# Column-tiled values and denominators in an attention and MLP kernel, with other first loads, a ring for the MLP input and warm-up matmuls

## The chip, the cores and the metric

The kernel runs on one core of a Trainium2 chip. The metric is the device time of one execution in microseconds (us); lower is better. The kernel before takes 539.99 us, the median of three runs (539.35 to 539.99).

## The reference

Eight sequences of 576 tokens go through attention with 8 heads of 64 and a bias that depends on the distance of two tokens (the bias table has 32 buckets for each head). The result, 4608 tokens of 512, goes through an MLP with a snake activation: 512 to 2048 and back to 512.

```python
scores = scale * np.matmul(q, k.transpose(0, 1, 3, 2))
scores = scores + bias_table[bucket].transpose(2, 0, 1)[None]
attn = np.exp(scores - max)
attn = attn / (np.sum(attn, axis=-1, keepdims=True) + 1e-09)
x = np.matmul(attn, v)              # heads side by side: 4608 x 512
h = x @ w_in
s = np.sin(alpha * h)
out = (h + s * s / (alpha + 1e-09)) @ w_out
```

## The kernel before

One stage per sequence t (0 to 7), in two parts. Scores are held transposed: keys on the partitions, queries along the row. In the code p is a pair of heads, z the head within the pair, w one of two windows of queries (384 and 192 wide) and c a chunk of 128 keys (c = 4 is the last 64 keys of both heads, stacked).

**Attention part.** For each pair p and window w, TensorE makes the scores (L472), ScalarE takes their exponential into u (L479), and VectorE multiplies the chunks near the diagonal by a table of exponentiated biases, m2 (L512), or mh for the last chunk (L495). Far from the diagonal the bias is one constant, which cancels. Then come values and denominators (L539): per head z, five matmuls over the key chunks. The stationary operand has 128 columns, 64 of values and 64 of ones, so that one accumulation gives the head's values on 64 rows and its denominator, copied 64 times, on the other 64. The two heads put them on opposite halves. ScalarE takes the logarithm of the denominators, one instruction of 64 rows per head (L553), and the exponential of its negative, one instruction of 128 rows (L566). VectorE multiplies the values by it into xT, one instruction of 64 rows per head (L574).

**MLP part.** A block b is 512 tokens; stage t does block t, and stage 7 does 7 and 8. For each of 16 groups f of 128 hidden units there are four matmuls (L600), a sine on ScalarE (L607), a square on ScalarE or VectorE (L614, L616), and the combination with h on VectorE into g (L621). The second matmul (L648, 64 per block, 16 for each of four outputs) needs a whole block of g. It is the fill: the planner puts its matmuls between the score matmuls of the next stage's attention. Exponential and sine need different tables on ScalarE, so each stage loads a table twice (L669).

**What sets the order.** Every engine works in its own order. A planner (class Plan) writes that order when the program is built: each task has costs, dependencies, a priority and, for some, an earliest time (T_V0, T_M2, T_W and so on), and the planner simulates the engines to choose. Fill matmuls are limited to QUOTA within the score matmuls of a stage. The simulated times choose the order only; on the chip an instruction waits for what it depends on.

**The start.** For t = 0 and t = 1 there is no time for the usual route of q and k (POOL writes them as f16 to DRAM, L273, and the DMA transposes them, L279 to L284). They are loaded with eight consecutive tokens in a row of 72 partitions (nat0 by SP at L321; nat1 and nat2 by POOL at L327 and L333), turned on TensorE (L396, L402) and copied out of PSUM by ScalarE or VectorE (L383, L385). In such a copy, neighbouring results go to places eight f16 elements apart, since eight tokens interleave. The bias table takes a chain: load the table (L314, L315), exponential (L350), a matmul with a 0/1 matrix phi_sb (L352), copy to e_sb (L353), and eight DMAs on SP that spread it over the partitions as m2, one per head (L355). VectorE builds mh from all heads of m2 (L372, L373). All the other loads go out on POOL's queue in the order of the program: q and k of t = 0, v of t = 0 (L291, L294), w_in (L301), q and k of t = 1, v of t = 1, and later w_out (L309), once the space of nat1 is free. The v tiles hold the ones beside the values, so that v is loaded in pieces of 64 columns.

## Time and profile before

| | |
|---|---|
| median of three runs | 539.99 us |
| the profiled execution | 541.17 us |
| its span, first to last instruction | 539.4 us |
| TensorE (matmul) busy | 452.9 us, 84% |
| ScalarE busy | 444.7 us, 82% |
| VectorE busy | 314.7 us, 58% |
| GpSimd busy | 100.6 us, 19% |
| first load of the exponential's table after stage 0 | at 124.08 us |
| the same after stage 6 | at 435.81 us |

A stage from 1 to 6 thus takes 51.96 us, stage 0 takes 124 us, and stage 7 with its two blocks takes 103.6 us. In the profile, a line number is one of the kernel before. A matmul's duration includes the way through the array, which the next matmul overlaps; how fast matmuls follow one another is read from a run of them. PE is TensorE, PEld its weight loads, ACT ScalarE, DVE VectorE, POOL GpSimd; SPq is the issuing of DMAs by SP.

### The profile page before, as it was taken

Reading aid. Unit: us, or ns where it says so; the run is one execution under the profiler, and the core shown is the slowest. Engines: PE = TensorE matmul, PEld = TensorE weight load, DVE = VectorE, ACT = ScalarE, POOL = GpSimd, SP = SyncE. Lnnn points to the kernel's source line nnn. Section 1 sums busy time; section 2 is a strip of 40 time slices with the busy share of each in tenths; the row PEclk is TensorE's granted clock in tenths of the full one; section 3 lists DMA queues with packets and bytes.
Section 4 is the critical chain, followed back from the end, with each engine's and each line's share of the span. In section 5 each row is a group of like instructions: output and inputs, shape, how many; then the busy total and the mean of one; then the engine's idle time right before and its main releaser. Section 6 shows DMA issues by size and latency. Waiting matters only on the chain.

```text
span 539.4 us, 7396 instructions
## 1 busy us (share of the span) xinstructions
PE 452.9 (84%) x2610; PEld 234.6 (43%) x2610; DVE 314.7 (58%) x613; ACT 444.7 (82%) x911; POOL 100.6 (19%) x114
## 2 busy tenths in 40 slices
PE   1414765399989998998999899979998999899997
PEld 0202442245544554454545444544554445444443
DVE  4623678276559555855675567557655765584800
ACT  3834777989989998999899989998998999895811
POOL 5334900710025004300520071005000000000000
PEclk9999776689999999999999999999999999999999
DMA  9999893990029904950694099309400000001022
GB/s 138 81 160 126 53 177 60 131 87 21 21 32 157 134 21 29 164 129 2 60 155 110 19 124 154 62 5 107 109 19 21 19 21 19 21 0 49 12 79 78
DMA packets 138977, 40.02 MB, mean 74 GB/s; under 512 B 125324, under 2 KB 133532, under 8 KB 138940
## 3 DMA queue, kind: packets, MB, share of 16 engines
q0 software_dynamic: 99072, 18.06, 44.1%
q1 hardware_dynamic: 39868, 21.49, 19.5%
q8 instruction: 20, 0.33, 0.3%
q14 instruction: 17, 0.14, 0.1%
HBM read 36.75 MB, written 16.52 MB: 99 GB/s over the span
## 4 chain that ended last, share of the span: by engine, by line
PE 53%; ACT 31%; DVE 6%; DMA 4%; SPq 3%; issue 2%; DVEq 0%; ACTq 0%
PE sc L600 24%; ACT u L479 20%; PE mo L648 14%; PE av L539 10%; PE sc L472 5%; ACT lnd L553 4%; SPq L355 3%; DMA m_73<-e_sb 3%; ACT rd L566 2%; ACT kz_67 L383 2%; DVE xT L574 2%; DVE kz_67 L385 2%; DMA phi_sb<-phi_const 1%; DVE u L512 1%; ACT L669 1%
## 5 line engine op out<-in xcount | busy, mean ns | idle before, releaser
L479 ACT ACTIVATE u<-sc 128x384 f16<-128x384 f32 x448 | 180.6, 503 | 3.1 <-PE sc L472 1.5
L648 PE MATMUL mo<-w_out_365,g 128*128 128x512 f16 x576 | 155.2, 379 | 0.0
L600 PE MATMUL sc<-xT,w_in_75 128*128 128x512 f16 x576 | 136.1, 386 | 6.3 <-DVE xT L574 6.3
L621 DVE SCALAR_TENSOR_TENSOR g<-sq,inv_a,sc 128x512 f16<-128x512 f16 x144 | 103.2, 745 | 17.0 <-ACT sq L614 7.5
L512 DVE TENSOR_TENSOR u<-u,m_73 128x512 f16<-128x512 f16 (+1 forms) x192 | 70.2, 392 | 66.7 <-ACT u L479 64.6
L574 DVE TENSOR_TENSOR xT<-av,rd 64x192 f16<-64x192 f32 (+1 forms) x128 | 58.2, 455 | 65.4 <-ACT rd L566 63.0
L600 PEld LDWEIGHTS <-w_in_75 128*128 128x128 f16 x576 | 57.0, 99 | 78.2 <-issue 16.8
L648 PEld LDWEIGHTS <-g 128*128 128x128 f16 x576 | 55.5, 97 | 64.4 <-issue 14.1
L472 PE MATMUL sc<-qT_69,kz_66 128*128 128x384 f16 (+1 forms) x288 | 65.5, 307 | 15.8 <-ACT u L479 15.3
L539 PE MATMUL av<-u,v_71 128*128 128x384 f16 (+1 forms) x320 | 56.2, 312 | 24.9 <-DVE u L512 21.1
L472 PE MATMUL sc<-qT_70,kz_67 128*128 128x384 f16 (+1 forms) x288 | 62.4, 284 | 12.1 <-ACT u L479 11.5
L553 ACT ACTIVATE lnd<-av 64x192 f32<-64x192 f32 (+1 forms) x128 | 51.8, 405 | 18.6 <-PE av L539 16.0
L291 POOL DMA_DIRECT2D v_72<-in_v_dram x32 | 24.0, 769 | 143.6 <-PE av L539 129.8
L539 PEld LDWEIGHTS <-v_71 128*128 128x128 f16 x320 | 31.2, 104 | 44.7 <-issue 30.1
L539 PE MATMUL av<-u,v_72 128*128 128x384 f16 (+1 forms) x320 | 49.3, 285 | 0.4 <-DVE u L512 0.2
L291 POOL DMA_DIRECT2D v_71<-in_v_dram x32 | 24.4, 788 | 114.8 <-PE av L539 110.3
L472 PEld LDWEIGHTS <-kz_66 128*128 128x128 f16 x288 | 28.9, 103 | 33.1 <-issue 20.6
L472 PEld LDWEIGHTS <-kz_67 128*128 128x128 f16 x288 | 27.4, 97 | 30.6 <-issue 16.4
L539 PEld LDWEIGHTS <-v_72 128*128 128x128 f16 x320 | 29.1, 97 | 18.3 <-issue 3.9
L383 ACT ACTIVATE outs<-mo 128x512 f32<-128x512 f32 x14 | 8.3, 595 | 26.2 <-PE mo L648 26.0
L566 ACT ACTIVATE rd<-lnd 128x384 f32<-128x384 f32 x64 | 27.9, 436 | 0.5
L383 ACT ACTIVATE kz_66<-mo 64x576 f16<-64x576 f16 (+2 forms) x5 | 10.9, 2269 | 19.0 <-DVE kz_66 L385 16.9
(345 smaller groups left out, 359.6 us busy)
## 6 DMA issues: line engine op xcount, KB each, us to landing
out_dram<-outs SPq DMA_DIRECT2D x36, 256.0 KB, 2.0
staged_k<-in_k_dram POOLq DMA_DIRECT2D x6, 576.0 KB, 9.5
staged_q<-in_q_dram POOLq DMA_DIRECT2D x6, 576.0 KB, 11.5
v_71<-in_v_dram POOLq DMA_DIRECT2D x32, 64.0 KB, 3.7
w_in_75<-in_moe_w_in_dram POOLq DMA_DIRECT2D x4, 512.0 KB, 17.1
v_72<-in_v_dram POOLq DMA_DIRECT2D x32, 64.0 KB, 5.4
w_out_365<-in_moe_w_out_dram POOLq DMA_DIRECT2D x4, 512.0 KB, 16.4
kz_66<-kraw SPq DMA_DIRECT2D x3, 288.0 KB, 3.6
```

Source lines behind the costliest of these rows:

```text
L291: nc.gpsimd.dma_start(out=dst[:, c], in_=vp[par, 128 * c : 128 * c + 128],)
L383: nc.scalar.activation(out=o, in_=i, func=AF.Copy)
L472: nc.tensor.matmul(out=sc.v[:, n * y : n * y + n], lhsT=kzs[t % 2][:, p, k0 : k0 + 128], rhs=qTs[t % 2][:, p, q0 : q0 + n], start=True, st ...
L479: nc.scalar.activation(out=u.v[:, k0 : k0 + nc_, q0 : q0 + n], in_=sc.v[:, 0 : n * nc_], func=AF.Exp, scale=0.125,)
L512: nc.vector.tensor_tensor(out=io, in0=io, in1=m2[:, 2 * p : 2 * p + 2, x0 : x0 + hi - lo], op=ALU.mult,)
L539: nc.tensor.matmul(out=avs[z].v[:, 0:n], lhsT=vs[t % 2][:, c, 2 * p + z, :, :], rhs=u.v[:, 8 if c == 4 else 4 * z + c, q0 : q0 + n], start ...
L553: nc.scalar.activation(out=ln.v[64 * z : 64 * z + 64, 0:n], in_=avs[z].v[64 - 64 * z : 128 - 64 * z, 0:n], func=AF.Ln,)
L566: nc.scalar.activation(out=rd.v[:, 0:n], in_=ln.v[:, 0:n], func=AF.Exp, scale=-1.0)
L574: nc.vector.tensor_tensor(out=xT[64 * z : 64 * z + 64, p, x0 : x0 + n], in0=avs[z].v[64 * z : 64 * z + 64, 0:n], in1=rd.v[64 * z : 64 * z ...
L600: nc.tensor.matmul(out=h.v, lhsT=w_in16[:, j, 128 * f : 128 * f + 128], rhs=xT[:, j, 512 * b : 512 * b + 512], start=(j == 0), stop=(j == 3),)
L621: nc.vector.scalar_tensor_tensor(out=gcell[b].v[:, f, :], in0=sq.v, scalar=inv_a[:, f : f + 1], in1=h.v, op0=ALU.mult, op1=ALU.add,)
L648: nc.tensor.matmul(out=m.v, lhsT=gcell[b].v[:, f, 128 * a : 128 * a + 128], rhs=w_out.v[:, f, :], start=(f == 0), stop=(f == NF - 1),)
```

## The change

1. **Bundles.** Per (t, p, w) there are two accumulations of both heads. The first gives the denominators on all 128 rows, the second the values. Each begins with a matmul of 128 columns for the stacked last chunk (ones2 or vh), and goes on with eight matmuls of 64 columns, alternately for the left and the right half of the array (z = 0, 1). A bundle is one task, and waits for all of its window's u. The logarithm becomes one instruction of 128 rows, and so does the multiplication into xT.
2. **First loads.** q and k of t = 0 and 1 have four tokens in a row: 128 partitions, and 16 for the last 64 tokens. A copy out of PSUM then writes four elements apart, and is two instructions (512 and 64 tokens). v needs no ones beside it and is loaded in six pieces instead of ten.
3. **Order of the loads.** phi_sb and the identity are loaded from ScalarE's queue. On POOL's queue come first pair 1 of q and k, the remainders, v, then pairs 2 and 3. Then POOL builds mh, and with it waits for m2; only behind it stand w_in, the loads for t = 1, and w_out, which has its own space now.
4. **Ring.** xT holds 1536 tokens instead of 4608; a multiplication that crosses the end is split.
5. **Warm-up.** Five matmuls on zeros ahead of the one of the bias table, and six behind it. The planner may add more in gaps; it adds none.
6. **Planner.** A change between bundles and other matmuls costs D_MODE there; fill has no gap, and its quota grows with the share of the scores done (8 + 48 times the share).

```diff
-        for z in range(2):
-            for c in range(4, -1, -1):
-                def mm(e, z=z, c=c):
-                    if c == 4:
-                        avs[z].v = new_av()
-                    nc.tensor.matmul(
-                        out=avs[z].v[:, 0:n], lhsT=vs[t % 2][:, c, 2 * p + z, :, :],
-                        rhs=u.v[:, 8 if c == 4 else 4 * z + c, q0 : q0 + n],
-                        start=(c == 4), stop=(c == 0),
-                    )
...
-            def lg(e, z=z):
...
-                nc.scalar.activation(
-                    out=ln.v[64 * z : 64 * z + 64, 0:n],
-                    in_=avs[z].v[64 - 64 * z : 128 - 64 * z, 0:n], func=AF.Ln,
-                )
+        for y in range(2):
+            def mm(e, y=y):
+                o = avs[y].v = new_av()
+                nc.tensor.matmul(
+                    out=o[:, 0:n], lhsT=vhs[t % 2][:, p] if y else ones2,
+                    rhs=u.v[:, 8, q0 : q0 + n], start=True, stop=False,
+                )
+                for c in range(4):
+                    for z in range(2):
+                        nc.tensor.matmul(
+                            out=o[64 * z : 64 * z + 64, 0:n],
+                            lhsT=vs[t % 2][:, c, 2 * p + z, :] if y else ones,
+                            rhs=u.v[:, 4 * z + c, q0 : q0 + n],
+                            start=False, stop=(c == 3),
+                        )
...
+            def lg(e):
+                ln.v = new_ln()
+                nc.scalar.activation(out=ln.v[:, 0:n], in_=avs[0].v[:, 0:n], func=AF.Ln)
...
-    SI = 8
-    SPB = S // SI
+    SI = 4
+    SN = (128, 16)
+    SO = (0, 512)
+    XN = 1536
...
+    nc.scalar.dma_start(out=phi_sb, in_=phi_h.ap())
+    nc.scalar.dma_start(out=id_sb, in_=idm.ap())
...
+    nc.gpsimd.tensor_copy(out=mh[0:64, :, :], in_=me[0:64, 0, :, 0:192])
+    nc.gpsimd.tensor_copy(out=mh[64:128, :, :], in_=me[64:128, 1, :, 64:256])
+    load_w_in16()
+    for kq, src in ((0, k), (1, q)):
+        load_nat([x[:, kq] for x in nat2], src[1], 0, H)
+    clear_v(nc.gpsimd, 1)
+    load_v16(1)
...
+    load_w_out16()
...
-FILL_GAP = 0.1
-QUOTA = 40
+D_MODE = 0.115
+FILL_GAP = 0.0
+QUOTA = 48
+OFFSET = 8
```

What stands on TensorE in a later stage. Before, values and denominators (L539, 128 columns) for the window of 192 stand between scores (L472) and fill (L648):

```order
L648 LDWEIGHTS g
L648 MATMUL mo<-w_out_365,g 128x512
L472 LDWEIGHTS kz_66
L472 MATMUL sc<-qT_69,kz_66 128x384
L539 LDWEIGHTS v_71
L539 MATMUL av<-u,v_71 128x192
```

Now a bundle begins; L607 is its matmul of 128 columns, L613 those of 64, of which eight follow one another:

```order
L541 LDWEIGHTS kz_67
L541 MATMUL sc<-qT_70,kz_67 128x384
L607 LDWEIGHTS ones_76
L607 MATMUL av<-u,ones_76 128x384
L613 LDWEIGHTS ones
L613 MATMUL av<-u,ones 64x384
```

And the place where the denominators' bundle ends and that of the values begins:

```order
L613 LDWEIGHTS ones
L613 MATMUL av<-u,ones 64x384
L607 LDWEIGHTS vh_74
L607 MATMUL av<-u,vh_74 128x384
L613 LDWEIGHTS v_72
L613 MATMUL av<-u,v_72 64x384
```

The matmuls of 128 columns that stood apart are now runs of eight of 64 columns, each run with one of 128 columns ahead of it. Of the 64 fill matmuls of a block, 61 stand among or ahead of the next stage's attention and 3 in the MLP part; before it was some 53 and 11.

POOL's queue at the start, before (v_71 and v_72 are v of t = 0 and 1, nat_89 is nat2):

```order
L294 DMA v_71<-in_v_dram 64x4x64 [waits DMASW3_49]
L301 DMA w_in_75<-in_moe_w_in_dram 128x2048 [waits DMASW4_49]
L301 DMA w_in_75<-in_moe_w_in_dram 128x2048 [waits DMASW5_49]
L301 DMA w_in_75<-in_moe_w_in_dram 128x2048 [waits DMASW6_49]
L301 DMA w_in_75<-in_moe_w_in_dram 128x2048 [waits DMASW7_49]
L333 DMA nat_89<-in_k_dram 72x8x512 [waits DMASW0_49]
```

And now (nat_128_95 is the part of nat1 with 128 partitions, nat_94 is nat2; DMAHW0 to 7 are the eight loads of m2):

```order
L346 DMA nat_128_95<-in_k_dram 128x4x256 [waits DMASW2_49]
L346 DMA nat_128_95<-in_q_dram 128x4x256 [waits DMASW3_49]
L413 COPY mh<-m_77 64x768 [waits DMAHW4_49,DMAHW6_49,DMAHW2_49,DMAHW0_49]
L414 COPY mh<-m_77 64x768 [waits DMAHW5_49,DMAHW7_49,DMAHW3_49,DMAHW1_49]
L354 DMA w_in_79<-in_moe_w_in_dram 128x2048 [waits DMASW4_49]
```

The load of w_in and all behind it now stand after the two copies that wait for m2.

286 lines of the change are left out of this document (164 added, 122 removed).

## The prediction

> **What bounds the kernel now.** The page first: two engines are busy over 80%, so the views by time must say which one ends the waits where.
>
> ```profile
> span 539.4 us, 7396 instructions
> PE 452.9 (84%) x2610; PEld 234.6 (43%) x2610; DVE 314.7 (58%) x613; ACT 444.7 (82%) x911; POOL 100.6 (19%) x114
> ```
>
> The chain that ended last, in order of time (start, length), marks the stages: L669 loads the exponential's table at the end of stage 0 and of stage 6.
>
> ```profile
> 28.08 15.90 DMA m_73<-e_sb
> 45.31 2.72 DVE kz_66 L385
> 101.43 2.71 ACT qT_70 L383
> 106.06 16.39 PE sc L600 x61
> 124.08 1.28 ACT L669
> 435.81 1.28 ACT L669
> 470.39 3.45 PE sc L600 x16
> 508.81 26.56 PE mo L648 x123
> 535.44 0.60 ACT outs L383
> ```
>
> So stage 0 takes 124.1 us, stages 1 to 6 take (435.81 - 124.08) / 6 = 51.96 each, and stage 7 takes 103.6. In stage 0 the chain is a DMA of m2 that ends at 44, then eleven copies of q and k out of PSUM between 45.31 and 104 (first and last shown), together 29.7.
>
> A later stage by the windows view (length, then busy PE, PEld, DVE, ACT, POOL): the MLP part of stage 3, then the attention part of stage 4.
>
> ```profile
> 209.60:227.40 17.80, 17.80 (x83) 8.02 (x82) 14.05 (x24) 17.45 (x29) 11.41 (x12) 1.00 1.52 130
> 227.40:261.90 34.50, 31.12 (x197) 17.85 (x195) 18.73 (x47) 31.78 (x79) 0.14 (x1) 1.00 0.39 67
> ```
>
> The MLP part fills TensorE and ScalarE alike. In the attention part ScalarE is busy 92%; TensorE's 31.1 contains latencies. Its real load comes from how matmuls follow one another (timeline and groups by shape):
>
> ```profile
> 65.95 0.57 PE L539 MATMUL av<-u,v_71 128*128 128x192 f16 x5
> 232.70 1.62 PE L539 MATMUL av<-u,v_72 128*128 128x384 f16 x9
> L539 PE MATMUL av<-u,v_72 128*128 128x384 f16 x160 | 31.0, 325 | 0.4 <-DVE u L512 0.2
> L539 PE MATMUL av<-u,v_72 128*128 128x192 f16 x160 | 18.3, 245 | 0.0
> ```
>
> Of 384 columns one follows another after (1.62 - 0.325) / 8 = 0.162, of 192 after (0.57 - 0.245) / 4 = 0.081, and of 512 after 26.56 / 123 = 0.216. A stage has 36 scores and 40 value matmuls of 384, as many of 192, and 128 of 512 (64 at L600, 64 at L648): 12.3 + 6.2 + 27.6 = 46.1. Of 51.96, TensorE idles 5.9, practically all in the attention part, where ScalarE paces it.
>
> **The bundles.** ScalarE and VectorE lose half of their instructions at L553 and L574:
>
> ```profile
> L553 ACT ACTIVATE lnd<-av 64x384 f32<-64x384 f32 x64 | 31.0, 485 | 5.1 <-PE av L539 3.7
> L553 ACT ACTIVATE lnd<-av 64x192 f32<-64x192 f32 x64 | 20.8, 325 | 13.5 <-PE av L539 12.2
> L574 DVE TENSOR_TENSOR xT<-av,rd 64x384 f16<-64x384 f32 x64 | 35.5, 555 | 43.4 <-ACT rd L566 42.4
> L566 ACT ACTIVATE rd<-lnd 128x384 f32<-128x384 f32 x32 | 16.5, 516 | 0.2
> ```
>
> L566 with 128 rows takes 516 ns, about what L553 takes with 64, so length counts, not rows. Per stage ScalarE saves 4 x (0.485 + 0.325) = 3.2; VectorE saves about as much, which it has to spare. If TensorE kept its load, the attention part would shrink by up to 3.
>
> TensorE does not. A bundle streams one matmul and four pairs, five lengths as before, if the halves of a pair run together. The nearest rows are the transposes at the start: L396 fills the array's columns, L402 alternates between its halves as L613 will.
>
> ```profile
> 11.70 0.66 PE L396 MATMUL mo<-id_sb,natx 72*128 72x72 f16 x8 [1.01 <-ACT natx L368]
> 16.84 0.69 PE L402 MATMUL mo<-id_sb,nat_90 72*64 72x72 f16 x16 [4.48 <-ACT qT_69 L383]
> 66.95 0.49 PE L472 MATMUL sc<-qT_69,kz_66 128*128 128x384 f16 x2
> 67.37 0.45 PE L402 MATMUL mo<-id_sb,nat_89 72*64 72x72 f16 x16
> 67.75 0.26 PE L472 MATMUL sc<-qT_69,kz_66 128*128 128x192 f16 x1
> ```
>
> Sixteen halves take 0.69 where eight whole ones take 0.66: the halves overlap fully. But entering and leaving costs. At 66.95 two matmuls of 0.162 would let the next start at 67.27; L402 starts at 67.37: 0.10. Its sixteen take about 16 x 0.015 = 0.24 at this clock, yet L472 starts 0.38 after them: 0.14. A bundle thus costs 0.23 (an estimate from these rows), and since every bundle has a whole matmul at its head, each of the 16 enters and leaves: 3.7 per stage. Bounds: 0.9, if the whole matmuls inside a group of bundles cost nothing (the order has four groups per stage), and 4.5, with leaving at both ends. I take 3.7, as the rows stand. The Trainium skill (TensorEngine Tiling, "Key Properties") says that a change of tiling mode drains TensorE; the trace agrees, with the 0.10 and 0.14. The same page ("Feature Incompatibilities") says that column tiling excludes fast weight loads, which speaks against this change: by "TensorE: Matmul & The Clock Gate" ("LDWEIGHTS") 64 columns then take an estimated 53 ns, and 128 of them unhidden would add 6.8 to a stage. The sixteen loads of L402 went by within those 0.38, so I take none.
>
> TensorE's load becomes 46.1 + 3.7 = 49.8, ScalarE's falls from 49.2 (17.45 + 31.78) to 46. TensorE now sets the attention part. It still waits at its head: for the table and the first exponential, and then at ScalarE's pace while two pairs of scores fill u.
>
> ```profile
> 227.42 1.28 ACT L669 ACT_TABLE_LOAD   x1
> 228.71 5.31 ACT L479 ACTIVATE u<-sc 128x384 f16<-128x384 f32 x14
> ```
>
> That is 1.28 + 0.4, and for 19 units at 5.31 / 14 = 0.38, 7.2 against 6.1 of matmuls placed there (19 scores, 14 fills): 1.1. Behind a bundle that waits for its last band stand scores and fills; the order puts other work ahead of most bundles, so I cost that at nothing, and at 8 x 0.38, one exponential each, at most. A stage takes 49.8 + 2.8 = 52.6, 0.6 more than now: what ScalarE saves, the changes of mode eat.
>
> **The tail.** Stage 7 runs 35 in attention (34.6 now). Now its end is full on TensorE: 298 matmuls from 470.39. After, the two blocks with only 6 fills among them are paced by ScalarE, 2 x 16 (17.45 without the table) + 2 to start; then come 121 fills at 0.216 = 26.1, of which 2 overlap, and 4.0 from the last matmul to the span's end: 62. Sum 97, against 103.6.
>
> **Stage 0.** Four rows from the timeline and eight-token copies by shape, beside a contiguous cast:
>
> ```profile
> 9.50 0.58 PE L352 MATMUL mo<-phi_sb,tabE 32*8 32x512 f16 x1 [9.50 <-DMA phi_sb<-phi_const]
> 10.73 17.95 SPq L355 DMA_DIRECT2D m_73<-e_sb  x8
> 42.22 0.35 DVE L372 COPY mh<-m_73 64x768 f16<-64x768 f16 x1 [12.00 <-DMA m_73<-e_sb]
> 45.16 3.04 PE L539 MATMUL av<-u,v_71 128*128 128x384 f16 x9 [15.12 <-DVE u L512]
> L385 DVE COPY kz_66<-mo 64x512 f16<-64x512 f16 x3 | 7.3, 2426 | 8.9 <-ACT kz_66 L383 8.9
> L385 DVE COPY kz_66<-mo 64x64 f16<-64x64 f16 x3 | 1.9, 649 | 0.0
> L366 DVE CAST natx<-natx 72x1024 f16<-72x1024 f32 x1 | 0.7, 692 | 1.8 <-DMA natx<-in_k_dram 1.8
> ```
>
> phi_sb from ScalarE's queue lets L352 start at about 5 instead of 9.5 (five warm-up matmuls of at most 0.58, 2.9 in all, end there too if they begin at 2), so the m2 loads begin 5 earlier. They also stop competing with w_in, which now waits behind them. Queue 0 in the DMA view, from 0 to 24, 24 to 30, 30 to 36 and 48 to 54 us (packets, MB, share):
>
> ```profile
> q0 software_dynamic: 5563, 1.48, 102.4%
> q0 software_dynamic: 677, 1.07, 96.9%
> q0 software_dynamic: 301, 0.96, 79.4%
> q0 software_dynamic: 3893, 0.53, 131.3%
> ```
>
> The first row is just q, k and v of t = 0 in f16; after the change m2 is alone from 24 on. I put its landing at 28 (22 to 44), and two copies on POOL at 1.0 each, between DVE's 0.35 and 1.5: mh at 30.5, not 44.4. Behind it at 1 MB per 6 us: w_in (2.1 MB) lands at 43, q and k of t = 1 at 51, v at 58, w_out at 71. Stage 0's MLP begins near 60 and its fill near 80, so these hide; if they fail, 72 is the floor of stage 0's end.
>
> Copies: 2.43 for 512 elements and 0.65 for 64 is 4 ns per element, against 0.7 ns in the cast. Eight f16 apart is one element per 16 bytes; four apart is two. The Trainium skill ("SBUF — State Buffer", "Door 1: The DMA port swizzle") names 16-byte lines that need two accesses each for full rate, though also a free step of 8 bf16, which these 4 ns contradict. By its full rate for two accesses a pair of copies would take the lower bound below, and the result would be 490. Bounds for a pair of copies: 0.65 (the cast's rate, twice the fixed part) and 3.1 (unchanged). I take 1.2. Eleven on the chain save 11 x 1.5 = 16.5. From mh to the table load it takes 79.6 now. Off come those 16.5; 3.2 at L553; 4.2, since eleven exponentials more (0.38) are done by then; and 3, half of what a faster clock gives the four windows of 384 (3.04 at 45.16, 1.62 at 232.70), since the array is kept warmer but not always. That leaves 52.7, and stage 0 ends at 30.5 + 52.7 = 83, a gain of 41. Ring, split multiplications, fewer v loads: nothing, on engines with idle time.
>
> **Sum.** 83 + 6 x 52.6 + 97 = 495.6 of span, against 539.4. The profiled execution lasted 541.17, 1.8 over its span, and 1.2 above the median of the runs: 495.6 + 1.8 - 1.2 = 496.
>
> **Rivals.**
> - *Interior changes are cheap* (0.9 per stage): 2.8 x 7 less, 476. For it: no row shows a change inside one accumulation. Against: 0.10 and 0.14 wherever a row does show one. 0.21.
> - *Copies stay slow*, because PSUM or the element count sets them: 11 x 1.9 more, 517. For it: VectorE and ScalarE take the same 2.7 (45.31, 101.43), so nothing in an engine sets it. The skill's free step of eight, above, would mean this: the spacing then never cost anything. 0.14.
> - *m2 lands late all the same* (44): its own queue is slow; 14 more, 510. For it: SP needed 17.95 to issue eight loads. 0.08.
> - *Slower: the halves don't overlap* at 384 columns. Then 16 x 4 streams per stage come in addition, 32 x (0.162 + 0.081) = 7.8; over eight stages 62: 558. It decides from 70% exposed on (44 of 62). Against: L402, at 72 columns. 0.04.
> - *Slower: the halves' weight loads are exposed.* A load of 128 columns takes 97 ns (below); half of it 128 times a stage is 6.2, over eight stages 50: 546. The skill's missing fast load, above, would do this. 0.02.
>
> ```profile
> L539 PEld LDWEIGHTS <-v_72 128*128 128x128 f16 x320 | 29.1, 97 | 18.3 <-issue 3.9
> ```
>
> My forecast has 0.5; 0.01 is for no change. The likeliest, 496, is the prediction. The range goes from 469 (cheap changes, and 7 of the 11 down to stage 0's floor) to 522 (slow copies, and 5 for later loads); the two slower cases and parts of two others, some 0.18, lie outside. Within 0.2%, about what measurement tells here, is 1.1 us: 0.01. Faster 0.93, slower 0.06.
>
> **What would show it.** Right: L629 at 64 instructions with 0.33 to 0.52 each; L448 and L450 at 0.5 to 1.5; mh near 30; the table load of stage 1 near 83; later stages at 52 to 53 with TensorE closer to full and ScalarE waiting for it. Wrong: runs of L613 that take over 0.1 per half at 384 columns, copies above 2, stages under 50.5, or w_out landing after 80 and holding the fill.

## The result and the profile after

The changed kernel takes 490.01 us (median of four runs, 489.17 to 491.33); the kernel before took 539.67 beside it (538.90 to 539.99). The ratio is 0.9084, with a 95% interval from 0.9061 to 0.9107: faster by 9.2%. The prediction said 496.0, with a range from 469 to 522. The profiled execution lasted 489.9 us, 1.8 more than its span.

The page of the changed kernel, with the span and each engine's busy time, share and instructions:

```profile
span 488.1 us, 8297 instructions
PE 456.9 (94%) x3133; PEld 229.1 (47%) x3133; DVE 277.5 (57%) x580; ACT 388.7 (80%) x838; POOL 83.3 (17%) x88
```

TensorE went from 84% to 94%, ScalarE lost 56 us of work and 73 instructions. The chain that ended last (start, length) has the marks of the stages; L738 loads a table, L414 is the second copy into mh, L717 the fill:

```profile
35.87 0.84 POOL mh L414
89.90 1.28 ACT L738
394.21 1.28 ACT L738
458.12 26.13 PE mo L717 x121
```

Stage 0 ends at 89.9 (before 124.1), stages 1 to 6 take (394.21 - 89.90) / 6 = 50.72 each (51.96), stage 7 takes 93.9 (103.6). So 34.2 of the 51.3 us of span come from stage 0, 7.4 from six stages, 9.7 from the last.

A later stage and the last one by the windows view (length, then busy time and instructions of PE, PEld, DVE, ACT, POOL; granted clock, DMA share, GB/s): MLP part of stage 2 and attention of stage 3, then attention, MLP part and rest of stage 7.

```profile
175.63:191.60 15.97, 15.97 (x75) 7.28 (x76) 14.00 (x24) 15.68 (x26) 9.24 (x8) 1.00 1.65 164
191.60:226.26 34.66, 34.52 (x271) 18.32 (x270) 16.06 (x41) 28.68 (x73) 0.00 (x0) 1.00 0.44 58
...
394.21:428.88 34.67, 34.52 (x272) 18.31 (x270) 16.07 (x41) 28.69 (x73) 0.00 (x0) 1.00 0.08 31
428.88:458.10 29.22, 29.22 (x136) 13.24 (x137) 27.00 (x46) 28.73 (x47) 0.00 (x0) 1.00 0.01 1
458.10:488.10 30.00, 26.13 (x122) 11.65 (x119) 2.15 (x4) 6.15 (x11) 0.00 (x0) 0.97 0.18 70
```

Before, ScalarE was busy 31.8 of the 34.5 us of such an attention part and TensorE 31.1; now it is 28.7 and 34.5. A share of 100% must be read with care, as the experiments show: a matmul's 0.33 us overlap the next one's 0.16, so a stall of up to 0.17 behind a matmul doesn't show.

The groups that answer to L553 and to the copies at L385 (busy time, mean ns, idle time before and its cause):

```profile
L629 ACT ACTIVATE lnd<-av 128x384 f32<-128x384 f32 x32 | 16.5, 515 | 23.8 <-PE av L613 23.8
L629 ACT ACTIVATE lnd<-av 128x192 f32<-128x192 f32 x32 | 10.7, 334 | 18.3 <-PE av L613 18.3
```

```profile
L450 DVE COPY kz_66<-mo 64x512 f16<-64x512 f16 x6 | 7.8, 1292 | 12.9 <-PE mo L470 7.7 <-ACT kz_66 L448 5.2
```

The logarithm of 128 rows takes 515 and 334 ns, with 64 rows it took 485 and 325: length counts, rows hardly. A copy of 512 elements takes 1.29 in place of 2.43.

The bundles in the timeline (start, length of the group; L607 has 128 columns, L613 is a half):

```profile
199.56 0.32 PE L607 MATMUL av<-u,ones_76 128*128 128x384 f16 x1
199.82 0.84 PE L613 MATMUL av<-u,ones 128*64 128x384 f16 x8
200.59 0.34 PE L607 MATMUL av<-u,vh_74 128*128 128x384 f16 x1
200.86 0.84 PE L613 MATMUL av<-u,v_72 128*64 128x384 f16 x8
201.63 0.26 PE L607 MATMUL av<-u,ones_76 128*128 128x192 f16 x1
```

From L607 to L607 it takes 1.03 and 1.04, that is five streams of 0.162 and 0.23. The whole matmul begins its halves 0.26 to 0.27 later (0.16 + 0.10 to 0.11), and eight halves need 0.77 (four streams of 0.162 and 0.12). The halves of a pair overlap fully at 384 columns, and the change of tiling costs 0.23 per bundle inside a group, too.

Stage 0, POOL and VectorE in the timeline (in brackets the idle time before, and who ended it):

```profile
34.74 0.82 POOL L413 COPY mh<-m_77 64x768 f16<-64x768 f16 x1 [23.77 <-DMA m_77<-e_sb]
```

```profile
36.73 0.26 DVE L564 TENSOR_TENSOR u<-u,mh 128x192 f16<-128x192 f16 x1 [7.41 <-POOL mh L414]
```

m2 lands at 34.7, not at 28, though w_in is out of its way. VectorE stands for 7.4 us at the multiplication by mh, with copies of k and q queued behind it. In the DMA view, m2 has the transfers nearly to itself from 24 to 30 us, 0.16 of 0.18 MB (packets, MB, share):

```profile
q1 hardware_dynamic: 221, 0.16, 73.1%
```

### The profile page after: what moved, and what is told of

It reads as the page before. It is cut to its first block, busy times and chain, and to the rows that moved or that the text cites. A ratio compares the mean times of both kernels' runs of the same rounds, so it can differ in the third digit from the quotient of the medians.

```text
span 488.1 us, 8297 instructions
## 1 busy us (share of the span) xinstructions
PE 456.9 (94%) x3133; PEld 229.1 (47%) x3133; DVE 277.5 (57%) x580; ACT 388.7 (80%) x838; POOL 83.3 (17%) x88
## 4 chain that ended last, share of the span: by engine, by line
PE 62%; ACT 24%; issue 6%; SPq 5%; DVE 1%; DMA 1%; POOL 0%; ACTq 0%; DVEq 0%
PE mo L717 20%; PE av L613 15%; PE sc L541 13%; PE sc L669 8%; PE av L607 5%; SPq L405 4%; ACT u L548 4%; ACT L738 3%; ACT sq L683 2%; DMA idf_sb<-identf 1%; PE mo L470 1%; ACT kz_67 L448 1%; SPq L410 1%; DVE kz_67 L450 1%; ACT rd L633 1%
## 5 line engine op out<-in xcount | busy, mean ns | idle before, releaser
L548 ACT ACTIVATE u<-sc 128x384 f16<-128x384 f32 x448 | 173.0, 544 | 17.9 <-PE sc L541 17.7
L717 PE MATMUL mo<-w_out_80,g 128*128 128x512 f16 x576 | 173.7, 379 | 0.0
L669 PEld LDWEIGHTS <-w_in_79 128*128 128x128 f16 x576 | 56.1, 99 | 69.3 <-issue 4.4
L717 PEld LDWEIGHTS <-g 128*128 128x128 f16 x576 | 55.7, 97 | 53.4 <-issue 4.3
L541 PE MATMUL sc<-qT_69,kz_66 128*128 128x384 f16 (+1 forms) x288 | 63.2, 298 | 1.0 <-ACT u L548 0.2
L541 PE MATMUL sc<-qT_70,kz_67 128*128 128x384 f16 (+1 forms) x288 | 63.7, 285 | 0.2
L629 ACT ACTIVATE lnd<-av 128x384 f32<-128x384 f32 x64 | 27.2, 425 | 42.0 <-PE av L613 42.0
L644 DVE TENSOR_TENSOR xT<-av,rd 128x384 f16<-128x384 f32 (+1 forms) x68 | 29.4, 437 | 48.6 <-ACT rd L633 32.6
L613 PE MATMUL av<-u,ones 128*64 128x192 f16 (+1 forms) x512 | 43.8, 293 | 0.0
L334 POOL DMA_DIRECT2D v_72<-in_v_dram x16 | 14.1, 889 | 131.1 <-PE av L613 124.8
L541 PEld LDWEIGHTS <-kz_66 128*128 128x128 f16 x288 | 26.5, 100 | 20.9 <-issue 5.0
L541 PEld LDWEIGHTS <-kz_67 128*128 128x128 f16 x288 | 26.7, 97 | 19.8 <-issue 0.8
L334 POOL DMA_DIRECT2D v_71<-in_v_dram x16 | 15.3, 1106 | 82.9 <-PE av L613 82.8
L450 DVE COPY outs<-mo 128x512 f32<-128x512 f32 x28 | 19.2, 687 | 17.7 <-PE mo L717 17.6
L613 PEld LDWEIGHTS <-ones 128*64 128x64 f16 x512 | 21.7, 109 | 13.4 <-issue 7.4
L613 PE MATMUL av<-u,v_71 128*64 128x384 f16 (+1 forms) x256 | 21.8, 292 | 0.0
L613 PE MATMUL av<-u,v_72 128*64 128x384 f16 (+1 forms) x256 | 21.8, 292 | 0.0
## 6 DMA issues: line engine op xcount, KB each, us to landing
staged_k<-in_k_dram POOLq DMA_DIRECT2D x6, 576.0 KB, 13.6
```

Source lines behind the costliest of these rows:

```text
L334: nc.gpsimd.dma_start(out=vs[t % 2][:, c], in_=vp[128 * c : 128 * c + 128],)
L541: nc.tensor.matmul(out=sc.v[:, n * y : n * y + n], lhsT=kzs[t % 2][:, p, k0 : k0 + 128], rhs=qTs[t % 2][:, p, q0 : q0 + n], start=True, st ...
L548: nc.scalar.activation(out=u.v[:, k0 : k0 + nc_, q0 : q0 + n], in_=sc.v[:, 0 : n * nc_], func=AF.Exp, scale=0.125,)
L613: nc.tensor.matmul(out=o[64 * z : 64 * z + 64, 0:n], lhsT=vs[t % 2][:, c, 2 * p + z, :] if y else ones, rhs=u.v[:, 4 * z + c, q0 : q0 + n] ...
L629: nc.scalar.activation(out=ln.v[:, 0:n], in_=avs[0].v[:, 0:n], func=AF.Ln)
L644: nc.vector.tensor_tensor(out=xT[:, p, (x0 + a) % XN : (x0 + a) % XN + m - a], in0=avs[1].v[:, a:m], in1=rd.v[:, a:m], op=ALU.mult,)
```

## Experiments

The stages of all kernels, from the exponential's table loads in their timelines; the last column is the median of the runs.

| kernel | stage 0 | stages 1-6, each | stage 7 | span | median |
|---|---|---|---|---|---|
| before | 124.1 | 52.0 | 103.6 | 539.4 | 539.7 |
| loadsalone | 94.8 | 52.0 | 103.4 | 510.2 | 512.3 |
| loadsfill | 96.5 | 52.1 | 94.7 | 503.6 | 505.5 |
| ln2 | 90.8 | 52.7 | 95.9 | 503.1 | 505.2 |
| actload | 89.8 | 51.5 | 94.7 | 493.6 | 496.1 |
| after | 89.9 | 50.7 | 93.9 | 488.1 | 490.0 |
| nowarm | 91.5 | 50.7 | 93.9 | 489.7 | 490.2 |
| ungated | 92.4 | 50.7 | 93.9 | 490.6 | 492.9 |
| heads | 90.0 | 53.7 | 96.0 | 508.3 | 509.4 |
| pure | 88.1 | 48.6 | 91.8 | 471.5 | 473.8 |
| turned | 82.0 | 48.6 | 91.9 | 465.5 | 469.2 |
| spread | 79.2 | 48.6 | 91.8 | 462.6 | 464.2 |
| best | 69.0 | 48.6 | 91.8 | 452.4 | 455.7 |

**heads: fewer changes of tiling, by order.** Both whole matmuls of a window first, then the sixteen halves.

```diff
-                o = avs[y].v = new_av()
-                nc.tensor.matmul(out=o[:, 0:n], lhsT=vhs[t % 2][:, p] if y else ones2, ...)
+                for g in range(0 if y else 2):
+                    avs[g].v = new_av()
+                    nc.tensor.matmul(out=avs[g].v[:, 0:n], lhsT=vhs[t % 2][:, p] if g else ones2, ...)
+                o = avs[y].v
```

> The change, with one edit: a pair's two matmuls of 128 columns (denominators, values) come first and the sixteen halves behind them, so TensorE changes its tiling twice per window instead of four times: 8 changes in and out less per stage. Theory (TensorE sets stages 1 to 7, and a change in and out costs 0.10 + 0.13 us): 8 x 0.23 = 1.85 less per stage, stages 1 to 6 at 48.8, and with the attention of stage 7 (1.85) and a part of stage 0 some 14 less in all: 476 us. Rival 1 (the change inside an accumulation is nearly free, and the 0.23 is something else at a bundle's head): 490, as after. Rival 2 (ScalarE takes over as the bound as soon as TensorE saves 1 us): about 482.

Measured: 509.39, ratio to before 0.9442 (0.9408 to 0.9476), 19 more than after. Neither the theory nor a rival had this. The waits of this kernel's TensorE (total, times, longest), with L611 the whole matmuls and L650 the multiplication into xT:

```profile
PE av L611 <- DVE xT L650: 21.3, 28, 1.0
```

After has no such wait. There are two av buffers. In the change, the denominators of the next window need only the first, which is free once the logarithm is taken; here both must be free, the second only after logarithm, exponential and multiplication. In the stage shown above, the first bundle of 192 columns starts 10.0 us behind the table load in after (201.63) and 12.2 in this kernel. The planner also put scores and fills in other places. So the run put a wait in the place of what it removed, and its time says nothing on the price of a change. Its timeline does: a window's two bundles of 384 with one change take 1.84 there (205.22 to 207.06), with two changes they take 2.07 in after. A stage lost 3.0 where 1.85 was to be gained; the 21.3 over eight stages are 2.7 of these 4.9. Short stalls behind matmuls don't show, and that rest stays open.

**ln2: two logarithms again.**

```diff
-                nc.scalar.activation(out=ln.v[:, 0:n], in_=avs[0].v[:, 0:n], func=AF.Ln)
+                for z in range(2):
+                    nc.scalar.activation(
+                        out=ln.v[64 * z : 64 * z + 64, 0:n],
+                        in_=avs[0].v[64 * z : 64 * z + 64, 0:n], func=AF.Ln,
+                    )
```

> The change, with the logarithm of the denominators as two instructions of 64 rows again. ScalarE gets 4 x (0.515 + 0.334) = 3.4 us more work per stage. Theory (TensorE sets the pace; ScalarE has that much idle time in each attention part): at most 2 us more in all, 490 to 492. Rival (ScalarE sets the pace, and its saving is where the gain of the later stages came from): 8 x 3.2 = 26 more, 516.

Measured: 505.15, ratio 0.9366 (0.9332 to 0.9400), 15 more than after. "TensorE sets the pace" fails as it was put. The attention part of the same stage in the windows view:

```profile
196.44:233.05 36.61, 35.64 (x272) 18.22 (x270) 16.07 (x41) 32.00 (x82) 0.00 (x0) 1.00 0.51 62
```

It takes 1.95 longer, with the same matmuls in the same order. Set beside after, matmul by matmul, the delay arises in two ways. Some 1.2 arise at scores (L541). They wait for exponentials, which stand behind the longer pair of logarithms on ScalarE, as here:

```profile
208.54 0.33 PE L541 MATMUL sc<-qT,kz 128*128 128x192 f16 x2 [0.16 <-ACT u L548]
```

Some 0.8 arise at bundles that wait for an av buffer: 0.1 at the denominators of each of the four windows of 192, behind the logarithms of the window ahead, and 0.4 at the values of the last one, behind its neighbour's multiplication. Stages 1, 2, 5 and 7 show the same places.

**actload: more work for ScalarE, off that chain.** An exponential of 64 rows into a tile that nobody reads, behind each exponential of denominators.

```diff
                 nc.scalar.activation(
                     out=rd.v[:, 0:n], in_=ln.v[:, 0:n], func=AF.Exp, scale=-1.0
                 )
+                nc.scalar.activation(
+                    out=spare[:, 0:n], in_=ln.v[0:64, 0:n], func=AF.Exp, scale=-1.0
+                )
```

> The change, with one more instruction on ScalarE behind each exponential of the denominators: 64 rows of the same length into a spare tile that nobody reads. ScalarE gets the same 3.4 us per stage as in the run with two logarithms, but not between a bundle and its multiplication. Theory 1 (what counts is the chain bundle, logarithm, exponential, multiplication, free buffer, next bundle): 490 to 493. Theory 2 (ScalarE's whole load sets the attention part together with TensorE's): about 505, the attention part at 36.6 as with two logarithms.

Measured: 496.06, ratio 0.9228 (0.9188 to 0.9268), 6.1 more than after; between the theories, and nearer to the chain's. Its attention part:

```profile
193.10:228.59 35.49, 35.27 (x272) 18.42 (x271) 16.19 (x42) 31.10 (x81) 0.19 (x1) 1.00 0.43 57
```

The load is less than was meant. ScalarE is busy 2.4 more than in after (31.10 for 28.68), in ln2 3.3 more, since the added exponential starts 0.43 behind the one ahead of it, which takes 0.52. Of the 0.8 that the attention part is longer, 0.6 arise where scores wait for exponentials, and 0.3 are the last added exponential, for which the next table load waits. So 6 us for 2.4 of work can't be set beside 15 for 3.3 as they stand; in proportion they would be 8.4. Both runs fit one reading: of the 15 us that the second logarithm costs, some 9 are ScalarE's time ahead of the exponentials (1.2 of the 2.0 per stage), and some 6 its place between a bundle and the buffer that a later bundle needs (0.8).

**loadsalone: the change without bundles**, and with the fill rule of before (logarithm and multiplication per head, ten whole matmuls per window).

```diff
-FILL_GAP = 0.0
-QUOTA = 48
-OFFSET = 8
+FILL_GAP = 0.1
+QUOTA = 0
+OFFSET = 40
...
-    vs = [sgl.tile([128, 4, H, D], F16, name=f"v{i}") for i in range(2)]
+    vs = [sgl.tile([128, 5, H, 2, D], F16, name=f"v{i}") for i in range(2)]
```

> The change without its first point: values and denominators as before (ten matmuls of 128 columns per window with ones beside the values, logarithm and multiplication per head, v in ten pieces), and the fill's gap and quota as before; first loads, order, ring and warm-up as in the change. Theory: stage 0 ends near 93 (3 later than after, for the logarithms), stages 1 to 6 at 52 as before, the tail at 103: 93 + 312 + 103 + 2 = 510, so that bundles give 20 of the 50 and the start 30. Rival, by the prediction's working (bundles give nothing in stages 1 to 6, and the start 41): stages at 52, but stage 0 at 86 and the tail at 97 to 103: 497 to 503. Rival 2 (the idle time at the head of the attention went with the copies or the ring, not with the bundles): stages at 50.7 here too, about 500 or less.

Measured: 512.27, ratio 0.9501 (0.9468 to 0.9535); 2 us over the theory's sum, and near it stage by stage.

**loadsfill: the same with the new fill rule.**

```diff
-FILL_GAP = 0.1
-QUOTA = 0
-OFFSET = 40
+FILL_GAP = 0.0
+QUOTA = 48
+OFFSET = 8
```

> As the run with the loads alone, but with the change's rule for the fill (no gap, quota 8 + 48 times the share). Theory 1 (the fill's new rule, and not the bundles, made the later stages and the tail shorter): stages 1 to 6 at 50.7, the tail at 94, 495 in all. Theory 2 (the rule needs the time that the one logarithm of 128 rows frees on ScalarE): attention parts at 36.5, MLP parts at 16, the tail at 96: 505 to 508.

Measured: 505.48, ratio 0.9391 (0.9359 to 0.9424), as theory 2 had it in all. What the rule changes is the tail; stages 1 to 6 stay at 52.1. The rest of stage 7 behind the attention in loadsalone, then in loadsfill:

```profile
442.16:510.20 68.04, 64.18 (x295) 28.59 (x293) 29.22 (x49) 37.19 (x61) 0.00 (x0) 0.99 0.12 43
```

```profile
444.34:503.60 59.26, 54.78 (x253) 24.47 (x251) 29.06 (x49) 35.31 (x58) 0.00 (x0) 1.00 0.10 36
```

There are 42 matmuls less behind the last attention: 42 x 0.216 = 9.1, of 8.8 measured. With this, four kernels part the gain of 49.7 us (the runs of before beside them had medians of 538.8 to 539.8): loads, order, ring and warm-up 27.4 (539.7 to 512.3), the fill rule 6.8 (to 505.5), bundles with two logarithms 0.3 (to 505.2), and the one logarithm of 128 rows, which only the bundles allow, 15.1 (to 490.0). The 0.3 is less than those medians differ, so these runs can't tell it from nothing. By the table it is a sum of opposites: from loadsfill to ln2, stage 0 is 5.7 shorter, each of stages 1 to 6 is 0.7 longer and stage 7 is 1.2 longer. No run shows why stage 0 gains.

**pure: bundles of halves only.** The whole matmul is written as two halves. The order then has 4 stretches of halves per stage, not 16.

```diff
-                nc.tensor.matmul(
-                    out=o[:, 0:n], lhsT=vhs[t % 2][:, p] if y else ones2,
-                    rhs=u.v[:, 8, q0 : q0 + n], start=True, stop=False,
-                )
+                for z in range(2):
+                    nc.tensor.matmul(
+                        out=o[64 * z : 64 * z + 64, 0:n],
+                        lhsT=vhs[t % 2][:, p, z] if y else ones2[:, z],
+                        rhs=u.v[:, 8, q0 : q0 + n], start=True, stop=False,
+                    )
```

> The change, with each bundle's matmul of 128 columns written as two halves of 64, so that a bundle is ten halves and neighbouring bundles are one stretch of halves: 4 stretches per stage in place of 16, in the same order otherwise. Theory (a change of tiling in and out costs 0.23 us, measured inside the bundles, and TensorE's time is on the path; the run with both wide matmuls ahead lost time because it needs both av buffers free at once): 12 x 0.23 = 2.8 less per stage at most; ScalarE, now the next in line, leaves 1.0 to 2.8 of it: stages 1 to 6 at 47.9 to 49.7, 470 to 482 in all. Rival (the lost time in the other run was the order of the matmuls, and the 0.23 is hidden behind ScalarE): 488 to 492.

Measured: 473.81, ratio 0.8805 (0.8779 to 0.8832), 16.2 less than after. A stage takes 48.6, 2.1 less for 12 changes of tiling less: 0.18 each of the 0.23. In the timeline (L608 is the pair that was one whole matmul) bundles follow one another without a gap:

```profile
193.61 0.35 PE L608 MATMUL av<-u,ones 128*64 128x384 f16 x2
193.80 0.82 PE L615 MATMUL av<-u,ones 128*64 128x384 f16 x8
194.45 0.33 PE L608 MATMUL av<-u,vh 128*64 128x384 f16 x2
194.61 0.82 PE L615 MATMUL av<-u,v 128*64 128x384 f16 x8
195.28 0.27 PE L608 MATMUL av<-u,ones 128*64 128x192 f16 x2
```

The values' bundle takes 195.28 - 194.45 = 0.83, five streams and 0.02. So the changes of tiling were on the path, and the prediction's rival that they cost nothing inside a group is out.

**ungated: w_in and the q and k of t = 1 ahead of the copies into mh again.**

```diff
+    load_w_in16()
+    for kq, src in ((0, k), (1, q)):
+        load_nat([x[:, kq] for x in nat2], src[1], 0, H)
     me = m2.rearrange("p (hp two) x -> p two hp x", two=2)
...
-    load_w_in16()
-    for kq, src in ((0, k), (1, q)):
-        load_nat([x[:, kq] for x in nat2], src[1], 0, H)
```

> The change, with w_in and the q and k of t = 1 put ahead of POOL's two copies again, so that they do not wait for m2. Theory (m2's eight loads are slow by themselves, about 26 GB/s, because each reads a single partition): m2 lands at 36 +- 1.5 as after, the exponential's table of stage 1 is loaded at 90 +- 1.5, 489 to 492 in all. Rival, as the prediction had it (w_in competes with m2): m2 lands about 8 later, at 44, and stage 0 and the total are 5 to 8 longer: 495 to 498.

Measured: 492.92, ratio 0.9144 (0.9106 to 0.9181). The copies into mh start at 36.88 in place of 34.74, and stage 0 ends at 92.4. So the order of the loads is worth 2 to 3 us. The prediction had m2 land 16 earlier, and put all but the 5 of the earlier phi_sb down to it.

**nowarm: without the eleven warm-up matmuls** (WARM0 and WARM1 at 0).

```diff
-    warm(WARM0)
...
-    warm(WARM1)
```

> The change without its eleven warm-up matmuls at the start. Theory (they keep the granted clock up for the first transposes and the bias row only, and m2 and the loads set stage 0): 490 to 491.5, the first exponential's table of stage 1 at 90 to 91. Rival, as the prediction had it (the warmer array gives 3 us in stage 0): 492 to 494, the table at 92 to 94.

Measured: 490.20, ratio 0.9100 (0.9064 to 0.9136): no difference that these runs can tell. The warm-up matmuls did not raise the clock either. The windows view prints 1.00 for the first 29 us, but the traces hold no record of the clock before 29.1 us in after and 34.0 in this kernel, and the pace of the matmuls says half. Six of the eleven, with 512 columns, in after:

```profile
4.89 2.73 PE L387 MATMUL mo<-kz_66 64*128 64x512 f16 x6
```

One follows another after (2.73 - 0.6) / 5 = 0.43, twice the 0.216 of the fill. The four scores of 384 columns at 13.6 us take 1.46 in both kernels, about 0.31 each, twice 0.162. What the eleven do is hold up the first transposes, shown for after (L463) and for this kernel (L461):

```profile
7.55 0.81 PE L463 MATMUL mo<-id_sb,natx 128*128 128x128 f16 x8
```

```profile
5.98 0.81 PE L461 MATMUL mo<-id_sb,natx 128*128 128x128 f16 x8 [1.55 <-DVE natx L426]
```

Without them the transposes start 1.6 earlier and take as long.

**probe: small measurements behind the end.**

```diff
     plan.run(T_START)
+    for run in range(5):
+        o = new_mo()
+        for i in range(8):
+            if run < 2 or run == 4:
+                nc.tensor.matmul(out=o[:, 0:384], lhsT=w, rhs=x, start=True, stop=True)
+            for j in range((0, 8, 8, 4, 2)[run]):
+                z = 0 if run == 3 else j % 2
+                nc.tensor.matmul(out=o[64 * z : 64 * z + 64, 0:384], lhsT=w[:, 64 * z : 64 * z + 64], rhs=x, ...)
+    for e in ("DVE", "ACT"):
+        for s in (1, 2, 4, 8, 16):
+            copy_on(e, d[0:64, 0:512].rearrange("d (p i) -> d i p", i=s),
+                    c[0:64, 0:512].rearrange("d (i p) -> d i p", i=s))
...
+    for g in range(5):
+        for i in range(4):
+            e = nc.scalar if g in (2, 3) and i > 1 else nc.sync
+            src = row(i + 2 if g == 3 and i > 1 else i, 0 if g == 1 else -1, 64 if g == 1 else 127)
+            e.dma_start(out=m2[:, i, :], in_=kzs[0][:, i, 0:XW] if g == 4 else src)
```

> The change, and behind its end a row of small measurements that nobody reads, so only its trace counts. TensorE, 384 columns: eight whole matmuls; eight times a whole one and eight halves; 64 halves by turns; 32 halves on one side; eight times a whole one and a pair of halves. Theory: 0.16 each whole, 1.04 each of the second kind, 0.16 a pair, 0.16 each on one side, 0.16 + 0.16 + 0.23 = 0.55 each of the last kind. Copies of 64 x 512 out of PSUM with results 1, 2, 4, 8, 16 f16 elements apart on VectorE and ScalarE: by the spacing theory (one access per 16 bytes from 8 apart on) about 0.6, 0.7 to 0.9, 1.3, 2.4, 2.4; rival (a smooth price per length of the inner run): 16 apart longer than 2.4. Loads of 128 rows of 768 bytes out of SBUF, four at a time: from single partitions on one queue as for m2 (expected 26 GB/s, 15 us); the same address for each row; two queues on neighbouring partitions; two queues on partitions 0, 1 and 4, 5; and from 128 partitions. Port theory: 26 GB/s in the first three, about twice in the fourth, over 100 in the fifth. Rival 1 (the shifted, odd addresses are slow): the second is faster. Rival 2 (the queue is slow): two queues are twice as fast on the same partitions, too.

TensorE in the timeline: a whole matmul and eight halves, the 104 halves of the second to fourth run, and a whole matmul with one pair.

```profile
486.57 0.84 PE L795 MATMUL mo<-kz 128*64 128x384 f16 x8
487.34 0.34 PE L792 MATMUL mo<-kz 128*128 128x384 f16 x1
487.61 0.84 PE L795 MATMUL mo<-kz 128*64 128x384 f16 x8
...
493.85 11.24 PE L795 MATMUL mo<-kz 128*64 128x384 f16 x104
505.02 0.34 PE L792 MATMUL mo<-kz 128*128 128x384 f16 x1
505.29 0.35 PE L795 MATMUL mo<-kz 128*64 128x384 f16 x2
505.57 0.34 PE L792 MATMUL mo<-kz 128*128 128x384 f16 x1
```

A whole one and eight halves repeat after 1.04, a whole one and a pair after 0.55; less 0.81 and 0.32 of streams, both leave 0.23. The 104 are 36 pairs and 32 halves on one side: (505.02 - 493.85) / 68 = 0.164 each, so a half alone costs as much as a pair.

What is paid at a change lies mostly ahead of the weight load, not in it. The first halves' load starts at 487.61, together with its matmul and 0.27 behind the whole one, though inside the run the loads start 0.16 ahead of theirs:

```profile
487.61 0.47 PEld L795 LDWEIGHTS <-kz 128*64 128x64 f16 x8 [0.17 <-issue]
```

The copies on VectorE, in groups for one instruction each, with results 1, 2, 4, 8 and 16 elements apart, then contiguous results from sources four apart:

```profile
L450 DVE COPY w_in<-av 64x512 f16<-64x512 f16 x1 | 0.4, 417 | 0.1
L450 DVE COPY w_in<-av 64x512 f16<-64x512 f16 x1 | 0.7, 722 | 0.0
L450 DVE COPY w_in<-av 64x512 f16<-64x512 f16 x1 | 1.3, 1286 | 0.0
L450 DVE COPY w_in<-av 64x512 f16<-64x512 f16 x1 | 2.4, 2432 | 0.0
L450 DVE COPY w_in<-av 64x512 f16<-64x512 f16 x1 | 2.3, 2320 | 0.0
L450 DVE COPY w_in<-av 64x512 f16<-64x512 f16 x1 | 0.7, 682 | 0.0
```

The price counts 16-byte pieces written: 64, 128, 256, 512, 512. From the first and the fourth, (2432 - 417) / 448 = 4.5 ns per piece, which gives 705 and 1281 for the second and third. ScalarE took 578, 738, 1312, 2451, 2372, and 590 for the last: from 128 pieces on 4.5 ns each, too, but less from 64 to 128. The Trainium skill ("SBUF — State Buffer", "Door 1: The DMA port swizzle") has 16-byte lines too, but a free step of up to 8 bf16; the measurement has none that is free.

The loads, in the DMA view: from single partitions (505 to 518 us, the same address for each row; with shifted addresses, as for m2, it was 26 GB/s from 490 to 503), from two queues at neighbouring partitions (521 to 535), and from two queues at partitions 0, 1 and 4, 5 (541 to 545).

```profile
DMA packets 507, 0.35 MB, mean 27 GB/s; under 512 B 48, under 2 KB 507, under 8 KB 507
...
DMA packets 522, 0.36 MB, mean 26 GB/s; under 512 B 48, under 2 KB 522, under 8 KB 522
...
DMA packets 314, 0.22 MB, mean 54 GB/s; under 512 B 33, under 2 KB 314, under 8 KB 314
```

Neither the shifted addresses nor the queue set the rate, but where the source lies. From 128 partitions the same four loads landed 2.0 us after their issue each. The Trainium skill (same section) gives four neighbouring partitions one port, with 27.6 GB/s measured; the trace agrees. It also says ("Can I just issue two DMAs to hit both halves?") that two transfers at once gain some 6%; here two with sources on different ports doubled the rate.

**turned: pure, with the copies turned inside out**, results contiguous.

```diff
-                    pin = c.v[:, o : o + SI * n].rearrange("d (i p) -> d i p", i=SI)
+                    pin = c.v[:, o : o + SI * n].rearrange("d (i p) -> d p i", i=SI)
...
-                        return tile[:, p, c0 : c0 + SI * n].rearrange("d (p i) -> d i p", i=SI)
+                        return tile[:, p, c0 : c0 + SI * n].rearrange("d (p i) -> d p i", i=SI)
```

> The run with pure halves, and the copies of q and k out of PSUM turned inside out: results contiguous, and sources 128 (or 16) elements apart, where before sources were contiguous and results four apart. Theory, from the small measurements (4.5 us per 1000 lines of 16 bytes written; strided sources 0.59 to 0.68): a copy of 64 x 512 at 0.45 to 0.8 in place of 1.29, eleven of them on the chain of stage 0, where a part of the time is a wait for m2: 3 to 6 less, 468 to 471. Rival (the source's distance costs as much as that of the results): copies at 1.3 or more, 473 to 475.

Measured: 469.21, ratio 0.8703 (0.8670 to 0.8736), 4.6 less than pure. The copies on VectorE and on ScalarE:

```profile
L450 DVE COPY kz<-mo 64x512 f16<-64x512 f16 x10 | 6.9, 691 | 15.9 <-PE mo L470 9.4 <-ACT kz L448 5.0 <-PE sc L541 1.5
```

```profile
L448 ACT ACTIVATE kz<-mo 64x512 f16<-64x512 f16 x6 | 3.5, 584 | 1.7 <-PE mo L470 1.6
```

**spread: pure, with each head's bias row on four partitions**, two ports by the Trainium skill ("SBUF — State Buffer", "Door 1: The DMA port swizzle"). A block-diagonal matmul makes the four shifted rows.

```diff
-            in_=bass.AP(tensor=e_sb.tensor, offset=e_sb[h : h + 1, 127:128].offset,
-                        ap=[[e_sb.ap[0][0], 1], [-1, 128], [1, XW]]),
+            in_=bass.AP(tensor=e_sb.tensor, offset=e_sb[4 * h : 4 * h + 1, 31:32].offset,
+                        ap=[[32 * e_sb.ap[0][0], 4], [-1, 32], [1, XW]]),
```

> The run with pure halves, and the row of biases of each head held on four partitions (32 s + 4 h, shifted by 32 for each s), so that a head's load reads four partitions in place of one. By the Trainium skill's port map (SBUF -- State Buffer, Door 1: The DMA port swizzle) these lie on two ports in place of one. Theory (the port of the source sets the rate of 27 GB/s): about 50 GB/s, m2 landed at 21 to 24 in place of 36, mh at 25 to 27 in place of 36.7; stage 0 then waits for the last loads of q and k and ends 5 to 10 earlier: 464 to 469 in all. Rival 1 (the rate belongs to the queue or to the rows' odd addresses): m2 at 35 to 37, 473 to 475. Rival 2 (m2 lands earlier, but the work of stage 0 and not m2 sets its end): less than 2 us gained, 472 to 474.

Measured: 464.17, ratio 0.8606 (0.8570 to 0.8642), 9.6 less than pure. POOL's copy into mh, and from 20 to 24 us what m2's queue moved:

```profile
24.37 0.82 POOL L426 COPY mh<-m 64x768 f16<-64x768 f16 x1 [13.14 <-DMA m<-e_sb]
```

```profile
q1 hardware_dynamic: 543, 0.38, 28.4%
```

m2 lands at 24.4, not 34.7, and stage 0 ends 8.9 earlier. Its 0.38 MB in 4 us are 95 GB/s, more than two ports' share (54 in probe); loads of several heads in flight at once may add up, which no run shows alone.

**best: pure, turned and spread together.**

> All three together: pure halves, turned copies, and m2 from four partitions per head. Theory: the copies' 4.6 (473.8 to 469.2) and m2's 9.6 (473.8 to 464.2) add up, since they shorten neighbouring pieces of stage 0: 459.5. If the copies were partly hidden behind the wait for m2, up to 2 more: 457.5. Rival (once m2 is early, the last loads of q and k set stage 0, and faster copies only wait for these): 462 to 464. Later stages at 48.5 in each case.

Measured: 455.65 (six runs, 454.22 to 456.52), ratio 0.8451 (0.8422 to 0.8479), below both kernels and below the 457.5 to 459.5 that were expected. Stage 0 takes 69.0; the copies save 10.2 there and not 6. The clock differs as well: the windows view has it granted at 0.50 twice in spread (35.0 to 38.4 and 58.9 to 62.3 us), and at 1.00 from 26 us on in best. That may be the rest, but no run tests it. TensorE is busy for 435.2 of the span's 452.4 us.

## Why the prediction was right

It forecast a faster kernel at 496.0; the span came out at 488.1 where the sum gave 495.6. The parts: stage 0 at 89.9 for 83 (+6.9), six stages at 50.72 for 52.6 (-11.3), stage 7 at 93.9 for 97 (-3.1). So the total is nearer than its parts, and that is luck. Of the way that the later stages would go, the sign was wrong: each was to take 0.6 more than before, and took 1.2 less.

- *The price of a change of tiling* (0.23 per bundle, 16 times a stage) is right, and inside a group too: 0.23 in the bundles, 0.23 twice in probe. The rival with cheap changes fell with them. No halves' weight load and no halved overlap showed: the two slower rivals needed them.
- *"What ScalarE saves, the changes of mode eat"* is what ln2 shows: with the changes, but without ScalarE's saving, a stage takes 52.7, beside 52.1 in loadsfill. But the saving is worth 2.0 per stage on top, which the prediction left out when it let TensorE set the attention part. TensorE doesn't set it alone. Three shares show: TensorE's streams and changes (pure: 2.1 per stage for 12 changes), ScalarE's time ahead of the exponentials (1.2 of ln2's 2.0), and the chain from a bundle by logarithm, exponential and multiplication to a free av buffer (the other 0.8). Waits behind a bundle were costed "at nothing"; with two logarithms they are not.
- *The idle 2.8 at the head of each stage* is the term that was mis-sized: 50.72 less the 49.8 of load leaves 0.9. In the timeline TensorE goes on with the fill (L717) while the table is loaded (at 191.60) and after:

```profile
191.00 1.03 PE L717 MATMUL mo<-w_out_80,g 128*128 128x512 f16 x4
191.86 0.33 PE L541 MATMUL sc<-qT_70,kz_67 128*128 128x384 f16 x1
192.03 0.81 PE L717 MATMUL mo<-w_out_80,g 128*128 128x512 f16 x3
```

The fill's new rule keeps these matmuls for the head, but the rule alone is not enough: loadsfill has it, and its stages take 52.1. With two logarithms (ln2, the same order of matmuls) TensorE idles 2.9 per stage, and what came in addition lies further on in the attention part, at the scores and buffers shown there.
- *The tail* had the right mechanism (only a few fills among the last two blocks' matmuls, loadsfill shows it). ScalarE's 2 x 16 + 2 was too much: the two blocks take 29.2, with TensorE busy all that time (136 matmuls) and ScalarE for 28.7. The rest takes 30.0 for 28.
- *m2 at 28* is the step of stage 0 that failed, "they also stop competing with w_in". m2 landed at 34.7 for 44 before. Of these 9.3, 5.1 are the earlier start of its loads (5.60 for 10.73), as forecast; the competition was worth 2 (ungated), not 11, and 2 stay open. What sets the rest is that its source lies on single partitions (probe, spread): eight loads of 98 KB at 27 GB/s are 29 us, from 5.60 on. The rival with a slow queue had a late m2, at 44, but not the cause: two queues on neighbouring partitions were no faster.
- *A pair of copies at 1.2* measured 1.43 in the timeline, within its bounds. The full rate for two accesses to a line, which would have given the lower bound, did not show: two results per 16 bytes took 1.29, contiguous ones 0.42 (probe).
- *From mh to the table load* it took 53.2, where 52.7 were forecast. That sum holds errors that cancel. The copies gave about 14 for 16.5 (1.43 a pair), and one logarithm in place of two gave 0.9 for 3.2 (ln2). The 3 for a warmer array was too small, if anything: the four windows of 384 took 3.04 each before, and about 2.07 in two bundles after, at the pace of the later stages. Nowarm shows that the warm-up matmuls are not what did it.

## What to carry to other kernels

Before a step is costed at an engine's load, look at what stands behind it in the engine's order, and at the chain that frees the buffer that the next step needs: 3.3 us more of ScalarE per stage cost 15 us ahead of both, and 2.4 us placed behind the chain cost 6. Matmuls of half width pay when they stand in long stretches: with 16 changes a stage and two logarithms the new tiling won nothing that the runs can tell, and 12 changes fewer won 16 us. A transfer that is slow while it is alone, and a copy that is slow on two engines alike, may be slow by where the bytes lie, as here: spreading the source over partitions won 9.6 us, writing contiguously 4.6. And a share or a clock that a view prints is worth a second look at the pace of the instructions themselves.

## What the runs showed of the hardware

- Loads out of one SBUF partition ran at 26 to 27 GB/s, and so did two queues at neighbouring partitions, whatever the addresses; with sources on partitions 0, 1 and 4, 5 two queues ran at 54.
- A copy's price went by the 16-byte pieces that it writes, 4.5 ns each on VectorE. Reading PSUM with a distance of 4 or 128 elements cost less: 0.68 to 0.69 on VectorE against 0.42 contiguous, and 0.58 to 0.59 on ScalarE against 0.58.
- A change from whole matmuls to halves and back cost 0.23, in three places. A half-width matmul on one side of the array took as long as a pair.
- Eleven matmuls over 5 us at the start ran at half pace to the last (0.43 for 512 columns), the scores behind them too, and the time without them was the same.
